# Regrouping the z2 projection of a gMLP layer: nine groups of eight 512-column units across row tiles, and a norm by VectorE alone

## The chip, the cores and the metric

The kernel runs on one core of one Trainium2 chip. A core has TensorE (PE, matrix products into PSUM), VectorE (DVE), ScalarE (ACT), GpSimd (POOL) and SyncE (SP, which issues DMA transfers here). The metric is the device time of one execution in microseconds (us). [...]

## The reference

Four layers run one after the other on a sequence of 2048 rows and 576 columns (D): attention (A), gMLP (B), A, B. Each takes the layer-normed input and adds its result to the stream. A is a dilated sliding-window attention and is not touched. B, with F = 4608 and Fh = 2304, is:

```python
z = gelu(x @ w_in)                      # 2048 x 4608, tanh form
z1 = z[..., :Fh]
z2 = layernorm(z[..., Fh:])             # mean and variance over the 2304 columns of a row
g = w_sp @ z2 + b_sp[:, None]           # w_sp is 2048 x 2048
out = (z1 * g) @ w_out                  # back to 576 columns
```

## The kernel before

A gMLP layer (`layer_B`) has three stages. The first, z2, computes the second half of z, its GELU and its layer norm into `Z`, by row tiles of 128 rows (16 of them). The second, `z1` and `gate`, goes over nine blocks (`jj`) of 256 columns: z1 transposed, and then the product of `Z` with the spatial weights `Wq`. The third projects back (`p3`).

The contraction over D = 576 is four chunks of 128 rows and one of 64. The 64-row chunk of two neighbouring 512-column units is done on the two row halves of the TensorE array at once (`tile_position`, rows 0 and 64; the last rows of the input and of the weights are there twice for it).

In the z2 stage `p1_main(i)` handles one row tile. Its 2304 columns are four units of 512 and one of 256. Two tiles of two PSUM banks (tag `H`, two buffers) take the four units, a one-bank tile (tag `PT`, four buffers) takes the 256 columns. The order on TensorE is: the four full chunks of units 0 and 1, then one block with the 64-row chunk of all five units, then the full chunks of units 2, 3 and 4. ScalarE then does three GELUs from PSUM into the row's buffer `zp` (three buffers), each with a running sum (L831). VectorE squares and sums columns 0 to 1535 (L833), ScalarE the other 768 (L835); the squares themselves go into `spare`, a scratch part of the `Z` tile, which lies where buffers of the layer before lay. Small VectorE operations make mean and variance (L838 to L846), POOL raises to the power -1/2 (L848) and makes -mean * rstd (L850).

`p1_norm(i)` writes the normed row into `Z`: VectorE the first 2048 columns (L858), POOL the last 256 (L860). It is called one row late. The tile framework puts the waits in and orders each engine's queue by readiness, so that a queue need not follow the program text; every engine then runs its queue in order.

Within the loop, transposes of the layer norm that the layer before left over (`run_deferred`) are issued ahead of the row that needs them. After row 2 SP issues four transposing loads of `B_w_sp` into `Wq` (L777) and the first w1 block (L799, L801; into `spare` too); after row 6 POOL issues the load of the bias (L873), into memory that held normed rows of the layer before.

The z1 stage (L887 to L926) has the order that matters for comparison: eight units of 512 columns per block, four in two `H` tiles and four in `PT` tiles, full chunks of the first four, one block with the 64-row chunks of all eight, full chunks of the last four. Its output tiles take over the memory of the z2 stage's pool. A `gate` call (L928) runs 16 matmuls over the row tiles of `Z` in order, into a `PT` bank.

Of the kernel before, what the change touches and what calls it, by code (L numbers as in the profile page):

```python
# [10 lines left out]
ALU = mybir.AluOpType  # L11
# [54 lines left out]
class K:  # L66
# [682 lines left out]
    def layer_B(self, li):  # L749
# [28 lines left out]
        cchunks = []  # L778
        c0 = 0
        while c0 < Fh:  # L780
            cn = min(1024, Fh - c0)
            cchunks.append((c0, cn))
            c0 += cn
        ncch = len(cchunks)
        SQ_D = (Fh * 2 // 3) // 256 * 256
        units = []
        for ci, (c0, cn) in enumerate(cchunks):
            for sub in range((cn + 511) // 512):
                units.append((ci, c0, sub, min(512, cn - sub * 512)))
# [12 lines left out]
        zst = {}  # L802

        def p1_main(i):
            zp = p1.tile([P, Fh], bf16, name="zp", bufs=3)
            sums = p1.tile([P, ncch + 2], f32, name="z_sums", bufs=3)
            pzvs = []
            for ci, (c0, cn) in enumerate(cchunks):
                if cn > 512:
                    pzvs.append(self.H_tile("pz")[:].rearrange("p a b -> p (a b)"))  # L810
                else:
                    pzvs.append(self.PT_tile([P, 512], f32, "pzs")[:, :])

            def z_mm(u, c, start, stop):
                ci, c0, sub, w = units[u]
                r0, r1 = (0, P) if c < 4 else (64 * (u % 2), 64 * (u % 2) + 64)
                nc.tensor.matmul(pzvs[ci][:, sub * 512:sub * 512 + w],  # L817
                                 lhsT=self.xnT[r0:r1, c, PADL + i * P:PADL + (i + 1) * P],
                                 rhs=win2(c)[r0:r1, c0 + sub * 512:c0 + sub * 512 + w],
                                 start=start, stop=stop, tile_position=(r0, 0))  # L820
            nu = len(units)
            for u in range(2):
                for c in range(4):
                    z_mm(u, c, c == 0, False)
            for u in range(nu):
                z_mm(u, 4, u >= 2, u < 2)
            for u in range(2, nu):
                for c in range(4):
                    z_mm(u, c, False, c == 3)
            for ci, (c0, cn) in enumerate(cchunks):  # L830
                nc.scalar.activation(out=zp[:, c0:c0 + cn], in_=pzvs[ci][:, 0:cn],  # L831
                                     func=ACT.Gelu_apprx_tanh, accum_out=sums[:, ci:ci + 1])
            nc.vector.tensor_tensor_reduce(out=spare[:, 0:SQ_D], in0=zp[:, 0:SQ_D], in1=zp[:, 0:SQ_D], scale=1.0,  # L833
                                           scalar=0.0, op0=ALU.mult, op1=ALU.add, accum_out=sums[:, ncch:ncch + 1])
            nc.scalar.activation(out=spare[:, SQ_D:Fh], in_=zp[:, SQ_D:Fh], func=ACT.Square,  # L835
                                 accum_out=sums[:, ncch + 1:ncch + 2])
            mean = p1.tile([P, 1], f32, name="z_mean", bufs=3)
            nc.vector.tensor_reduce(out=mean[:], in_=sums[:, 0:ncch], axis=AX.X, op=ALU.add)  # L838
# [4 lines left out]
            sq = p1.tile([P, 1], f32, name="z_sq", bufs=3)  # L843
            nc.vector.tensor_tensor(out=sq[:], in0=sums[:, ncch:ncch + 1], in1=sums[:, ncch + 1:ncch + 2], op=ALU.add)
# [17 lines left out]

        for i in range(NS):
            self.run_deferred(upto_row=(i + 1) * P)
            p1_main(i)
            if i == 0:
                self.run_deferred()
            if i == min(2, NS - 1):
# [216 lines left out]
```

## Time and profile before

| what | us |
|---|---|
| median of 3 runs | 1184.68 (1182.94 to 1186.77) |
| the profiled execution | 1182.29 |
| its span | 1180.5 |
| TensorE busy | 1169.8 |
| z2 of the first gMLP layer, first matmul to first z1 matmul | 127.93 to 204.56 |
| z2 of the second | 709.94 to 786.12 |
| one z1 block with its gates | 35.6 |

In the timelines the columns are start and duration in us, engine, line, operation, output and inputs, array rows and columns, shape, count; in brackets the idle time of the engine ahead of the instruction and what ended it. Matmuls overlap in the record (each is listed with 379 ns for 512 columns, though one starts every 216 ns), so distances between starts are used, not durations. The profiled execution is one; the median is over others.

### The profile page before, as it was taken

The numbers are of one execution on the slowest core, as the hardware profiler recorded it, in microseconds if no ns is written. First come the engines' busy times: TensorE is split into PE (matmuls) and PEld (weight loads), VectorE is DVE, ScalarE is ACT, GpSimd is POOL, SyncE is SP. The second block draws the span as 40 slices with busy tenths as digits, with TensorE's granted clock in tenths as the row PEclk, the third lists the DMA queues.
The fourth block names the chain that finished last, engine by engine and source line by source line (L and its number), as shares of the span: only waits on it lengthen the run. The fifth ranks groups of instructions, "written<-read, shape, count | busy, mean of one in ns | idle before, by whom it ended". The sixth has DMA issues, their size and how long they took to land.

```text
span 1180.5 us, 20534 instructions
## 1 busy us (share of the span) xinstructions
PE 1169.8 (99%) x8406; PEld 622.2 (53%) x8406; DVE 553.0 (47%) x1232; ACT 377.3 (32%) x621; POOL 285.8 (24%) x383
## 2 busy tenths in 40 slices
PE   9999999999999999999999999999999999999998
PEld 5567544444444444457755774444444444444677
DVE  9778677323333322335556896753322333332321
ACT  5588677111110111102257786770111110111000
POOL 4768784000000000001153787830000000000000
PEclk9999999999999999999999999999999999999999
DMA  8999993000000000049645899900000000001332
GB/s 200 199 136 235 197 206 70 23 12 12 12 1 12 12 12 1 18 145 282 170 99 116 201 245 175 223 23 1 12 12 12 12 3 10 12 1 39 114 106 74
DMA packets 179479, 101.57 MB, mean 86 GB/s; under 512 B 135711, under 2 KB 160735, under 8 KB 179384
## 3 DMA queue, kind: packets, MB, share of 16 engines
q1 hardware_dynamic: 166520, 78.50, 31.2%
q0 software_dynamic: 6512, 16.00, 5.2%
q10 hardware_dynamic: 6352, 5.75, 1.6%
q8 instruction: 66, 1.08, 0.4%
q14 instruction: 29, 0.24, 0.1%
HBM read 42.39 MB, written 16.53 MB: 50 GB/s over the span
## 4 chain that ended last, share of the span: by engine, by line
PE 89%; POOL 4%; DMA 2%; DVE 2%; issue 1%; ACT 1%; SPq 0%; POOLq 0%; ACTq 0%; DVEq 0%
PE pg L931 42%; PE po L973 12%; PE pz L817 9%; PE pz L907 6%; PE pz1s L907 6%; PE pp L409 4%; PE pv L386 2%; PE O_ps L464 2%; PE L_ps L444 2%; POOL ln_xn L245 2%; PE pw L509 2%; PE pzs L817 1%; DMA o_slot<-o_t 1%; DMA QK<-win2a 1%; POOL QK L80 1%
## 5 line engine op out<-in xcount | busy, mean ns | idle before, releaser
L931 PE MATMUL pg<-Wq,Z 128*128 128x512 bf16 x2304 | 500.2, 379 | 0.0
L931 PEld LDWEIGHTS <-Z 128*128 128x128 bf16 x2304 | 225.4, 98 | 271.9
L935 DVE TENSOR_TENSOR g_tmp<-pg,ln_xn 128x512 f32<-128x512 f32 x144 | 99.6, 692 | 422.2 <-PE pg L931 422.2
L926 ACT ACTIVATE z1T<-pz 128x1024 bf16<-128x1024 f32 x36 | 34.9, 1020 | 497.4 <-PE pz L907 493.8
L80 POOL DMA_DIRECT2D wout<-in_B_w_out_dram x4 | 4.2, 1062 | 600.8 <-PE pg L931 600.8
L973 PE MATMUL po<-wout,Z 128*128 128x288 bf16 x1152 | 141.4, 286 | 0.0
L453 ACT ACTIVATE P_sb<-L_ps 128x912 bf16<-128x912 f32 (+1 forms) x144 | 125.7, 929 | 36.2 <-PE L_ps L444 35.3
L973 PEld LDWEIGHTS <-Z 128*128 128x128 bf16 x1152 | 112.7, 98 | 28.8
L817 PEld LDWEIGHTS <-xnT 128*128 128x128 bf16 (+1 forms) x800 | 66.5, 97 | 83.3 <-issue 25.6
L936 DVE TENSOR_TENSOR Z<-g_tmp,z1T 128x512 bf16<-128x512 f32 x144 | 99.7, 692 | 13.0 <-DVE g_tmp L935 0.9
L817 PE MATMUL pz<-win2a,xnT 128*128 128x512 bf16 x384 | 104.1, 380 | 1.5 <-ACT zp L831 1.5
L907 PEld LDWEIGHTS <-w 128*128 128x128 bf16 (+1 forms) x640 | 53.8, 97 | 74.0 <-issue 13.6
L409 PE MATMUL pp<-xnT,wqk_sb 128*128 128x512 bf16 x360 | 82.5, 379 | 0.0
L831 ACT ACTIVATE zp<-pz 128x1024 bf16<-128x1024 f32 x64 | 65.5, 1023 | 36.8 <-PE pz L817 31.1
L983 DVE TENSOR_TENSOR x_new<-po,xo 128x288 f32<-128x288 f32 (+1 forms) x64 | 28.8, 456 | 87.7 <-PE po L973 84.0
L907 PE MATMUL pz<-xnT,w 128*128 128x512 bf16 (+1 forms) x320 | 66.5, 380 | 0.0
L907 PE MATMUL pz1s<-xnT,w 128*128 128x512 bf16 (+1 forms) x320 | 66.5, 379 | 0.0
L817 PE MATMUL pz<-win2b,xnT 128*128 128x512 bf16 (+1 forms) x256 | 65.7, 380 | 0.0
L80 POOL DMA_DIRECT2D QK<-stg x81 | 50.9, 633 | 50.9 <-DVE oT L483 17.9
L833 DVE CUSTOM_DVE_ANT_0 Z<-zp 128x1536 bf16<-128x1536 bf16 x32 | 56.9, 1778 | 11.5 <-ACT zp L831 7.1
L386 PE MATMUL pv<-wv_sb,xnT 128*128 128x288 bf16 (+1 forms) x360 | 52.8, 286 | 1.1 <-DVE o_t L471 1.0
L245 POOL TENSOR_SCALAR ln_xn<-x_new,ln_mv,ln_rstd 128x576 bf16<-128x576 f32 x23 | 53.0, 2303 | 2.0
(118 smaller groups left out, 1002.2 us busy)
## 6 DMA issues: line engine op xcount, KB each, us to landing
xres<-x_new SPq DMA_DIRECT2D x48, 288.0 KB
xo<-xres SPq DMA_DIRECT2D x32, 288.0 KB
wout<-in_B_w_out_dram POOLq DMA_DIRECT2D x4, 1296.0 KB, 8.6
xo<-xres SPq DMA_DIRECT2D x8, 576.0 KB
w<-in_B_w_in_dram SPq DMA_DIRECT2D x16, 256.0 KB
QK<-stg POOLq DMA_DIRECT2D x53, 72.0 KB, 4.3
QK<-stg SPq DMA_DIRECT2D x41, 72.0 KB
xo<-in_A_x_dram SPq DMA_DIRECT2D x8, 288.0 KB
```

The source lines that it names most:

```text
L80: return eng.dma_start(out=out, in_=in_)
L245: e.tensor_scalar(out=xn[:nrows, 0:D], in0=x_t[:nrows, :], scalar1=mv[:nrows, 0:1], scalar2=rstd[:nrows, 0:1], op0=ALU.subtract, op1=ALU.mult)
L386: nc.tensor.matmul(pv[:nk, 0:288], lhsT=self.xnT[:, c, KO + q0_(t):KO + q0_(t) + nk], rhs=wv_sb[:, c, hh * 288:(hh + 1) * 288], start=(c = ...
L409: nc.tensor.matmul(pp[:, :], lhsT=w, rhs=self.xnT[:, c, PADL + cc * 512:PADL + (cc + 1) * 512], start=(c == 0), stop=(c == 4))
L453: nc.scalar.activation(out=P_bufs[(2 * s + jp) % 4][:nk, :, :, 0:nq], in_=Lv[:nk, :, :, 0:nq], func=ACT.Exp, scale=scale)
L817: nc.tensor.matmul(pzvs[ci][:, sub * 512:sub * 512 + w], lhsT=self.xnT[r0:r1, c, PADL + i * P:PADL + (i + 1) * P], rhs=win2(c)[r0:r1, c0 + ...
L831: nc.scalar.activation(out=zp[:, c0:c0 + cn], in_=pzvs[ci][:, 0:cn], func=ACT.Gelu_apprx_tanh, accum_out=sums[:, ci:ci + 1])
L907: nc.tensor.matmul(outs[a_], lhsT=w1[r0:r1, c, sub * P:(sub + 1) * P], rhs=self.xnT[r0:r1, c, PADL + q * 512:PADL + (q + 1) * 512], start= ...
L931: nc.tensor.matmul(pg[:, :], lhsT=Z[:, jj, i, sub * P:(sub + 1) * P], rhs=Wq[q][:, i, :], start=(i == 0), stop=(i == NS - 1))
L935: nc.vector.tensor_tensor(out=tmp[:], in0=pg[:, :], in1=bsp[:, qs], op=ALU.add)
L936: nc.vector.tensor_tensor(out=uT(jj)[:, sub, qs], in0=tmp[:], in1=z1Ts[jj, sub][:, qs], op=ALU.mult)
L973: nc.tensor.matmul(acc[hh], lhsT=uT(j // 2)[:, j % 2, i * P:(i + 1) * P], rhs=wouts[j // NJH][:, j % NJH, hh * 288:(hh + 1) * 288], start= ...
```

## The change

The z2 stage no longer goes row by row. For each pair of row tiles the units are put in a row: four units of 512 columns of the first row, one merged unit ("m") that holds the last 256 columns of both rows side by side in one bank, and four units of the second row. The 72 units are taken eight at a time (`groups`), whatever rows they belong to. A group has two `H` tiles with two neighbouring units each, and four `PT` tiles. `p1_group` does the full chunks of the four `H` units, those of the merged unit's first row, one block with all 64-row chunks (the merged unit's two parts on the same row half, one after the other), and the full chunks of the `PT` units, with the merged unit's second row.

The GELUs follow the units, so a row has up to four or five with a running sum each. ScalarE squares only the 256 columns of the merged unit (`SQ_D` is now 2048), VectorE the other 2048, for the last row in two parts. The factor 1/Fh goes into the squares, and the two sums are added in the last small operation. VectorE norms all 2304 columns in one operation; POOL keeps only the power. Statistics of a row are issued when its last unit is done, the norm one row later. The loads of `Wq` and w1 follow group 1, the bias load follows group 3, and all left-over transposes are issued after group 0.

```diff
--- before.py
+++ after.py
@@ -775,18 +775,7 @@
 
         def load_W(q):
             nc.sync.dma_start_transpose(out=Wq[q][:], in_=self.B_w_sp[q * 512:(q + 1) * 512, :])
-        cchunks = []
-        c0 = 0
-        while c0 < Fh:
-            cn = min(1024, Fh - c0)
-            cchunks.append((c0, cn))
-            c0 += cn
-        ncch = len(cchunks)
-        SQ_D = (Fh * 2 // 3) // 256 * 256
-        units = []
-        for ci, (c0, cn) in enumerate(cchunks):
-            for sub in range((cn + 511) // 512):
-                units.append((ci, c0, sub, min(512, cn - sub * 512)))
+        SQ_D = Fh - 256
         bsp = self.bsp
         w1_0 = spare[:, Fh:Fh + 1280].rearrange("p (c n) -> p c n", n=256)
         p2s = []
@@ -799,81 +788,120 @@
             self.dma(w1[:, 0:4, :], self.B_w_in[0:512, cs].rearrange("(c p) n -> p c n", p=P), eng=nc.sync)
             for r in (0, 64):
                 self.dma(w1[r:r + 64, 4, :], self.B_w_in[512:576, cs], eng=nc.sync)
-        zst = {}
-
-        def p1_main(i):
-            zp = p1.tile([P, Fh], bf16, name="zp", bufs=3)
-            sums = p1.tile([P, ncch + 2], f32, name="z_sums", bufs=3)
-            pzvs = []
-            for ci, (c0, cn) in enumerate(cchunks):
-                if cn > 512:
-                    pzvs.append(self.H_tile("pz")[:].rearrange("p a b -> p (a b)"))
-                else:
-                    pzvs.append(self.PT_tile([P, 512], f32, "pzs")[:, :])
-
-            def z_mm(u, c, start, stop):
-                ci, c0, sub, w = units[u]
-                r0, r1 = (0, P) if c < 4 else (64 * (u % 2), 64 * (u % 2) + 64)
-                nc.tensor.matmul(pzvs[ci][:, sub * 512:sub * 512 + w],
-                                 lhsT=self.xnT[r0:r1, c, PADL + i * P:PADL + (i + 1) * P],
-                                 rhs=win2(c)[r0:r1, c0 + sub * 512:c0 + sub * 512 + w],
-                                 start=start, stop=stop, tile_position=(r0, 0))
-            nu = len(units)
-            for u in range(2):
+        zst, zrow = {}, {}
+        npair, MW = Fh // 1024, Fh % 1024
+        assert MW == 256 and NS % 2 == 0
+        stream = []
+        for r in range(0, NS, 2):
+            stream += [(r, w_) for w_ in range(2 * npair)] + [("m", r)] + [(r + 1, w_) for w_ in range(2 * npair)]
+        groups = [stream[k_:k_ + 8] for k_ in range(0, len(stream), 8)]
+        left = {r: 2 * npair + 1 for r in range(NS)}
+
+        def unit_parts(u):
+            if u[0] == "m":
+                return [(u[1], 2 * npair * 512, 0, MW), (u[1] + 1, 2 * npair * 512, MW, MW)]
+            return [(u[0], u[1] * 512, 0, 512)]
+
+        def z_mm(u, out, c, half, start, stop, part=0):
+            r0, r1 = (0, P) if c < 4 else (64 * half, 64 * half + 64)
+            for r, w0, o0, n in unit_parts(u)[part:part + 1]:
+                nc.tensor.matmul(out[:, o0:o0 + n], lhsT=self.xnT[r0:r1, c, PADL + r * P:PADL + (r + 1) * P],
+                                 rhs=win2(c)[r0:r1, w0:w0 + n], start=start, stop=stop, tile_position=(r0, 0))
+
+        def p1_group(units):
+            pairs = [k_ for k_ in range(len(units) - 1) if units[k_][0] != "m" and units[k_][1] % 2 == 0 and
+                     units[k_ + 1] == (units[k_][0], units[k_][1] + 1)][:2]
+            first = [units[k_ + a_] for k_ in pairs for a_ in range(2)]
+            rest = [u for u in units if u not in first]
+            outs, acts = {}, []
+            for k_ in pairs:
+                ht = self.H_tile("pz")[:].rearrange("p a b -> p (a b)")
+                for a_ in range(2):
+                    outs[units[k_ + a_]] = ht[:, a_ * 512:(a_ + 1) * 512]
+                acts.append((units[k_][0], units[k_][1] * 512, ht, 2))
+            for u in rest:
+                outs[u] = pt = self.PT_tile([P, 512], f32, "pzs")[:, :]
+                for r, w0, o0, n in unit_parts(u):
+                    acts.append((r, w0, pt[:, o0:o0 + n], 1))
+            for u in first:
                 for c in range(4):
-                    z_mm(u, c, c == 0, False)
-            for u in range(nu):
-                z_mm(u, 4, u >= 2, u < 2)
-            for u in range(2, nu):
+                    z_mm(u, outs[u], c, 0, c == 0, False)
+            single = [u for u in first + rest if u[0] != "m"]
+            merged = [u for u in rest if u[0] == "m"]
+            for u in merged:
                 for c in range(4):
-                    z_mm(u, c, False, c == 3)
-            for ci, (c0, cn) in enumerate(cchunks):
-                nc.scalar.activation(out=zp[:, c0:c0 + cn], in_=pzvs[ci][:, 0:cn],
-                                     func=ACT.Gelu_apprx_tanh, accum_out=sums[:, ci:ci + 1])
-            nc.vector.tensor_tensor_reduce(out=spare[:, 0:SQ_D], in0=zp[:, 0:SQ_D], in1=zp[:, 0:SQ_D], scale=1.0,
-                                           scalar=0.0, op0=ALU.mult, op1=ALU.add, accum_out=sums[:, ncch:ncch + 1])
-            nc.scalar.activation(out=spare[:, SQ_D:Fh], in_=zp[:, SQ_D:Fh], func=ACT.Square,
-                                 accum_out=sums[:, ncch + 1:ncch + 2])
+                    z_mm(u, outs[u], c, 0, c == 0, False)
+            for k_, u in enumerate(single):
+                z_mm(u, outs[u], 4, k_ % 2, u in rest, u in first)
+            for u in merged:
+                for k_ in range(2):
+                    z_mm(u, outs[u], 4, 1, k_ == 1, k_ == 0, k_)
+            for u in rest:
+                for c in range(4):
+                    z_mm(u, outs[u], c, 0, False, c == 3, 1 if u[0] == "m" else 0)
+            done = []
+            for r, w0, src, n in acts:
+                if r not in zrow:
+                    zrow[r] = [p1.tile([P, Fh], bf16, name="zp", bufs=3),
+                               p1.tile([P, 2 * npair + 4], f32, name="z_sums", bufs=3), 3]
+                zp, sums, k_ = zrow[r]
+                zrow[r][2] += 1
+                w = src.shape[-1]
+                nc.scalar.activation(out=zp[:, w0:w0 + w], in_=src, func=ACT.Gelu_apprx_tanh,
+                                     accum_out=sums[:, k_:k_ + 1])
+                if w0 == SQ_D:
+                    nc.scalar.activation(out=spare[:, SQ_D:Fh], in_=zp[:, SQ_D:Fh], func=ACT.Square,
+                                         scale=Fh ** -0.5, accum_out=sums[:, 0:1])
+                left[r] -= n
+                if left[r] == 0:
+                    done.append(r)
+            return done
+
+        def p1_stats(i):
+            zp, sums, n = zrow.pop(i)
+            cuts = [0, SQ_D // 2, SQ_D] if i == NS - 1 else [0, SQ_D]
+            for k_, (q0, q1) in enumerate(zip(cuts, cuts[1:])):
+                nc.vector.tensor_tensor_reduce(out=spare[:, q0:q1], in0=zp[:, q0:q1], in1=zp[:, q0:q1], scale=1.0 / Fh,
+                                               scalar=0.0, op0=ALU.mult, op1=ALU.add, accum_out=sums[:, 1 + k_:2 + k_])
+            if len(cuts) > 2:
+                nc.vector.tensor_tensor(out=sums[:, 1:2], in0=sums[:, 1:2], in1=sums[:, 2:3], op=ALU.add)
             mean = p1.tile([P, 1], f32, name="z_mean", bufs=3)
-            nc.vector.tensor_reduce(out=mean[:], in_=sums[:, 0:ncch], axis=AX.X, op=ALU.add)
+            nc.vector.tensor_reduce(out=mean[:], in_=sums[:, 3:n], axis=AX.X, op=ALU.add)
             nc.vector.tensor_scalar_mul(out=mean[:], in0=mean[:], scalar1=1.0 / Fh)
             msq = p1.tile([P, 1], f32, name="z_msq", bufs=3)
             nc.vector.scalar_tensor_tensor(out=msq[:], in0=mean[:], scalar=mean[:, 0:1], in1=self.eps_t[:],
                                            op0=ALU.mult, op1=ALU.subtract)
-            sq = p1.tile([P, 1], f32, name="z_sq", bufs=3)
-            nc.vector.tensor_tensor(out=sq[:], in0=sums[:, ncch:ncch + 1], in1=sums[:, ncch + 1:ncch + 2], op=ALU.add)
             rstd = p1.tile([P, 1], f32, name="z_rstd", bufs=3)
-            nc.vector.scalar_tensor_tensor(out=rstd[:], in0=sq[:], scalar=1.0 / Fh, in1=msq[:],
-                                           op0=ALU.mult, op1=ALU.subtract)
+            nc.vector.scalar_tensor_tensor(out=rstd[:], in0=sums[:, 0:1], scalar=sums[:, 1:2], in1=msq[:],
+                                           op0=ALU.add, op1=ALU.subtract)
             nc.gpsimd.tensor_tensor(out=rstd[:], in0=rstd[:], in1=self.neg_half[:], op=ALU.pow)
-            nmr = p1.tile([P, 1], f32, name="z_nmr", bufs=3)
-            nc.gpsimd.tensor_scalar(out=nmr[:], in0=mean[:], scalar1=rstd[:, 0:1], scalar2=-1.0,
-                                    op0=ALU.mult, op1=ALU.mult)
-            zst[i] = (zp, mean, rstd, nmr)
+            zst[i] = (zp, mean, rstd)
 
         def p1_norm(i):
-            zp, mean, rstd, nmr = zst.pop(i)
-            nb = NB - 1
+            zp, mean, rstd = zst.pop(i)
             zv = zp[:].rearrange("p (b c) -> p b c", c=256)
-            nc.vector.tensor_scalar(out=Z[:, 0:nb, i, :], in0=zv[:, 0:nb, :], scalar1=mean[:, 0:1],
+            nc.vector.tensor_scalar(out=Z[:, 0:NB, i, :], in0=zv, scalar1=mean[:, 0:1],
                                     scalar2=rstd[:, 0:1], op0=ALU.subtract, op1=ALU.mult)
-            nc.gpsimd.tensor_scalar(out=Z[:, nb, i, :], in0=zv[:, nb, :], scalar1=rstd[:, 0:1],
-                                    scalar2=nmr[:, 0:1], op0=ALU.mult, op1=ALU.add)
-
-        for i in range(NS):
-            self.run_deferred(upto_row=(i + 1) * P)
-            p1_main(i)
-            if i == 0:
+
+        waiting = []
+        for k_, units in enumerate(groups):
+            self.run_deferred(upto_row=(max(r for u in units for r, _, _, _ in unit_parts(u)) + 1) * P)
+            done = p1_group(units)
+            if k_ == 0:
                 self.run_deferred()
-            if i == min(2, NS - 1):
+            if k_ == 1:
                 for q in range(NQ):
                     load_W(q)
                 load_w1(0)
-            if i == min(6, NS - 1):
+            if k_ == 3:
                 self.dma(bsp, self.B_b_sp.partition_broadcast(P), eng=nc.gpsimd)
-            if i >= 1:
-                p1_norm(i - 1)
-        p1_norm(NS - 1)
+            for r in done:
+                p1_stats(r)
+                waiting.append(r)
+                if len(waiting) > 1:
+                    p1_norm(waiting.pop(0))
+        while waiting:
+            p1_norm(waiting.pop(0))
         p1_cm.__exit__(None, None, None)
         self.right["pf_cm"].__exit__(None, None, None)
         self.right = None
```

## The prediction

> **What bounds the kernel now.** I read the page first: busy shares, then the chain of waits, then the windows and timelines of the two z2 stages.
>
> ```profile
> PE 1169.8 (99%) x8406; PEld 622.2 (53%) x8406; DVE 553.0 (47%) x1232; ACT 377.3 (32%) x621; POOL 285.8 (24%) x383
> PE 89%; POOL 4%; DMA 2%; DVE 2%; issue 1%; ACT 1%; SPq 0%; POOLq 0%; ACTq 0%; DVEq 0%
> ```
>
> TensorE is the path (89% of the chain). "99% busy" hides what matters, since matmuls overlap in this record; the distance from one start to the next is what counts. So I read z2 as steps of the chain, beside z1 (the next stage), which already works in the pattern that the change brings to z2. Columns: start, us, what.
>
> ```profile
> 153.68 2.27 PE pz L817 x12
> 156.05 1.83 PE pz L817 x8
> 158.32 2.27 PE pz L817 x12
> ...
> 204.72 3.99 PE pz L907 x20
> 208.71 3.99 PE pz1s L907 x20
> ```
>
> A row of z2 takes 158.32 - 153.68 = 4.64 us and holds one block of 64-row matmuls. A z1 step has eight 512-column units and also one such block, and takes 3.99 + 3.99 = 7.98 us. Inside a row (TensorE's timeline):
>
> ```profile
> 164.31 0.38 PE L817 MATMUL pz<-win2b,xnT 128*128 128x512 bf16 x1
> 164.62 0.61 PE L817 MATMUL pz<-win2b,xnT 64*128 64x512 bf16 x4
> 165.06 0.27 PE L817 MATMUL pzs<-win2b,xnT 64*128 64x256 bf16 x1
> 165.27 0.82 PE L817 MATMUL pz<-win2a,xnT 128*128 128x512 bf16 x3
> 166.14 0.81 PE L817 MATMUL pz<-win2a,xnT 128*128 128x512 bf16 x3
> ```
>
> Four full matmuls take 166.14 - 165.27 = 0.865, so a slot of 512 columns is 0.216 us. From the last full start (164.31) to the first 64-row start (164.62) is 0.31: entering the block costs 0.095 beyond the slot. From 165.06 to 165.27 is 0.21 for a matmul of 256 columns (0.108): leaving costs another 0.10. Between, two pairs side by side take 0.44. Each block thus costs about 0.20 us of switching.
>
> Two waits also lie on the path, one per layer:
>
> ```profile
> 139.60 0.81 PE L817 MATMUL pz<-win2a,xnT 128*128 128x512 bf16 x3 [0.98 <-ACT zp L831]
> 137.61 0.84 ACT L835 ACTIVATE Z<-zp 128x768 bf16<-128x768 bf16 x1 [2.55 <-DMA xnT<-stg]
> 730.45 0.81 PE L817 MATMUL pz<-win2a,xnT 128*128 128x512 bf16 x3 [0.53 <-ACT zp L831]
> 729.28 1.02 ACT L831 ACTIVATE zp<-pz 128x1024 bf16<-128x1024 f32 x1 [1.96 <-DVE z_sq L844]
> 727.29 1.95 POOL L860 TENSOR_SCALAR Z<-zp,z_rstd,z_nmr 128x256 bf16<-128x256 bf16 x1
> ```
>
> In the first layer ScalarE's Square waits for a transpose out of memory that `spare` takes over; the GELU behind it frees the next PSUM tile late. In the second, GELU of row 3 waits for the `zp` buffer of row 0, which VectorE and then POOL's norm (727.29 + 1.95 = 729.24) still hold. By start times TensorE loses 1.1 and 0.7 us there.
>
> **The change part by part.** The sum is against the profiled execution, 1182.29 us (span 1180.5 and 1.8 around it). The median shown is 1184.68, or 2.39 more, which I add at the end.
>
> *TensorE, steady.* Before, a row is 20 slots of 512, a lone 64-row matmul of half a slot, and a block: 20.5 x 0.216 + 0.20 = 4.63 (4.64 seen); 16 rows are 74.24 us. After, a group has 32 full slots (the merged unit's are eight of 256 columns) and four pairs: the seventh 512 unit lies beside the two halves of the merged one. 36 x 0.216 + 0.20 = 7.98, which is z1's own time. Nine groups: 71.8. Saved 2.4 us a layer: four slots (0.87) and seven blocks (1.4). Matmuls stay 400 a layer, weight loads too (98 ns under slots of 108 or 216). Bounds on the merged unit: 0, as it fits z1's pattern, to one more slot in eight groups (1.7 a layer) if its halves do not run beside the 512. I take 0: the lone 64-row matmul of 256 columns before starts 0.21 after the pair ahead and costs no extra slot.
>
> [...]
>
> *The first wait.* Group 0 ends at 127.93 + 1.23 (output matmuls of the layer before, in between) + 7.98 = 137.1. ScalarE reaches the first Square near 136.4 and stays blocked to 137.6. Behind it are Square 0.47, the second half's GELU 0.5, Square 0.47, and three GELUs of 512 (0.60 apart in z1, which reads no accumulator; 0.66 with one, an estimate from 0.97 and 1.00 for 1024): the one-bank tiles come free at 138.7, 139.8, 140.5, 141.2. Group 1 first needs such a bank 16 slots in, at 140.6 (that of 139.8), the last at 141.8. TensorE waits 0; bounds 0 and today's 1.1. I take 0.3, as the margins are under a microsecond.
>
> *The second wait.* POOL's norm of 256 columns goes (32 x 0.56 to 1.95 us, POOL only), with L850's 0.79. Row 3 now waits for row 0's VectorE norm alone. POOL's power came at 725.71, behind the bias DMA of L873, which waits for the last transpose; the norm then ends near 727.3, and ScalarE would want the buffer about 727.2. What is late next is VectorE's backlog of three rows, which reaches the one-bank GELUs of group 2. Bounds 0 and 1.2; I take 0.5.
>
> *VectorE.* Sum of squares: 1.68 start to start for 1536, so 2.24 in proportion for 2048, a little less if part is fixed; I take 2.2. Small operations 1.0, less the `z_sq` add: 0.78. Norm 0.73 for 2048, between 0.73 and 0.82 for 2304; 0.80. Together 3.8 a row, or 4.45 if it waits each time for POOL's power (0.67 from the last small operation to the norm, in all 32 rows). A row's share of a group is 71.8 / 16 = 4.49. So it is hidden, thinly.
>
> *ScalarE.* A group: two GELUs of 1024 (1.0 each), three of 512 (0.66), two of 256 (0.5), two Squares (0.47, between 0.38 and 0.84): 5.9 us of 7.98. It ends some 2.7 after TensorE's group, and the next group needs the last bank after 3.46: margin 0.75.
>
> *End of a stage.* Row 15 is complete 2.5 us after TensorE leaves z2. Two sums of 1.15, small operations, power and two norms put its Z at about +7 us (+5 today). The first gate reads row 15 at 7.98 + 15 x 0.216 = +11.2. Row 14's norm ends at about +6.3, which may hold the third z1 GELU 0.4 us if its output takes over that row's buffer; the gate's bank has 1.5 us. Cost 0, bounds 0 and 1.5.
>
> *DMA issues.* SP's four transposes of `B_w_sp` and three loads of w1 move from after row 2 (13.9 us in) to after group 1 (16.0); they filled SP from 141.7 to 183.9, and the gate starts near 209. The last row's transpose moves past group 0, but POOL finishes its input at 139.6, later than that. POOL's bias load moves from after row 6 (32.5 us) to after group 3 (31.9). All cost nothing.
>
> Sum: layer 1, -2.4 - 1.1 + 0.3 = -3.2; layer 2, -2.4 - 0.7 + 0.5 = -2.6. Total -5.8, of which I keep -5.7, leaving 0.1 to the stage ends: 1176.6 profiled, 1179.0 median.
>
> **The rivals.**
> (1) VectorE's in-order queue eats part of the gain: two rows now complete together, and a norm waits behind the next row's 2.2 us sum while a GELU needs that `zp` buffer (three exist). For: the margins of 0.75 and of 4.49 against 4.45. Against: 3.8 if the power is covered. A norm behind a whole sum and its small operations is 3.0 late, 2.2 beyond the margin; once a layer that is 4.4, less the 0.8 of waits counted already: 1182.6.
> (2) Slower, by one mechanism: POOL's power is held while VectorE works. POOL's 256-column norm took 0.56 alone and 1.95 beside the sum of squares. If the norm of a row always waits for such a power, a row costs 4.45 plus the hold. Up to 4.49 it is free; at 4.7 z2 takes 75.3, as today with its waits (74.24 + 1.1 and + 0.7), and beyond that it is slower. With half a microsecond of hold it is 4.95, or 79.2 a layer, 3.9 and 4.3 over today: 1192.9. Against: no power waited so far, and the next row's small operations can cover it. [...]
> (3) The merged unit's halves do not pair: +1.7 a layer, 1182.4.
>
> **How the numbers follow.** Forecast 0.66, rival 1 0.14, rival 2 0.10, rival 3 0.10. A measurement can tell about 0.3% (3.6 us) from no change. The forecast with waits at their lower bounds gives -6.6 (1178.1); two microseconds for the spread of the runs give 1176. Above, it runs with the upper bounds of the waits (+1.5), the stage end (+1) and that spread to 1184, where rivals 1 and 3 lie; 1185 leaves rival 2. Faster takes most of the forecast and little of rivals 1 and 3 (0.70), same the rest of these (0.18), slower rival 2 and a little of rival 1 (0.12).
>
> **What would show it.** Groups of z2 7.98 apart; z1 starting 3.2 and then 5.8 us earlier; 18 blocks of 64-row matmuls in both z2 stages together, not 32; no POOL norm; no wait of TensorE over 0.6 in z2. It is wrong if z2's groups are over 8.2 apart, if TensorE waits for GELUs, or if the first gate halts at row 14 or 15.

## The result

The changed kernel takes 1202.0 us (median of five runs, 1200.9 to 1205.2), the kernel before 1184.77 (five runs beside it, 1182.9 to 1186.8). The ratio is 1.0147, with a 95% interval of 1.0127 to 1.0167: slower by 17 us, where the prediction said 1179.0, between 1176 and 1185. The profiled execution took 1200.93 us, with a span of 1199.1.

The page of the changed kernel, its busy line and its chain of waits by engine:

```profile
PE 1172.0 (98%) x8406; PEld 624.0 (52%) x8406; DVE 583.0 (49%) x1206; ACT 359.8 (30%) x677; POOL 215.9 (18%) x319
...
PE 77%; DVE 11%; POOL 5%; DMA 2%; ACT 2%; issue 2%; POOLq 0%; DVEq 0%; ACTq 0%
```

TensorE's work is what it was (1172.0 us busy against 1169.8, as many matmuls), but its share of the chain fell from 89% to 77%, and VectorE's rose from 2% to 11%. POOL is relieved as announced (215.9 us, before 285.8). Where VectorE came into the chain is seen in the groups by line and in the chain of the end of the first z2 stage (columns: start, us, what):

```profile
L883 DVE TENSOR_SCALAR Z<-zp,z_mean,z_rstd 128x2304 bf16<-128x2304 bf16 x32 | 46.4, 1470 | 24.1 <-POOL z_rstd L877 24.1
```

```profile
199.10 2.20 DVE Z L864
...
202.29 0.56 POOL z_rstd L877
...
202.87 1.47 DVE Z L883
204.35 2.20 DVE Z L864
...
207.46 0.56 POOL z_rstd L877
...
208.05 1.47 DVE Z L883
209.52 2.20 DVE Z L864
...
215.33 1.48 DVE Z L883
...
216.89 2.44 ACT z1T L954 x3
219.33 0.04 issue
219.37 2.72 PE pg L959 x6
```

The norm of 2304 columns takes 1.470 us a time. The norm of 2048 took 0.813 in the kernel before:

```profile
L858 DVE TENSOR_SCALAR Z<-zp,z_mean,z_rstd 128x2048 bf16<-128x2048 bf16 x32 | 26.0, 813 | 31.0 <-POOL z_rstd L848 31.0
```

A row on VectorE is now a serial loop: sum 2.20, small operations, POOL's power (0.73 with the way there and back), norm 1.47, and then the next sum; from 199.10 to 204.35 is 5.25, from 204.35 to 209.52 is 5.17. TensorE, where nothing holds it, delivers a row every 4.5 us (a group starts at 138.82 and the next at 146.82 in the run with the even cut below, 8.00 us for 16/9 of a row). So VectorE falls behind through the stage, its norm of row 14 ends at 216.8, ScalarE's first z1 GELU starts right behind it, and the first gate starts when the third of these GELUs (2.44 us for the three) has freed its PSUM bank.

TensorE's timeline at the end of the first stage in the kernel before, and at both ends in the changed kernel (in brackets the idle time ahead, and what ended it):

```profile
212.54 27.79 PE L931 MATMUL pg<-Wq,Z 128*128 128x512 bf16 x128
240.17 4.16 PE L907 MATMUL pz<-xnT,w 128*128 128x512 bf16 x20
```

```profile
205.60 4.16 PE L935 MATMUL pz<-xnT,Z 128*128 128x512 bf16 x20
209.59 4.15 PE L935 MATMUL pz1s<-xnT,Z 64*128 64x512 bf16 x20
219.37 29.73 PE L959 MATMUL pg<-Wq,Z 128*128 128x512 bf16 x128 [5.63 <-ACT z1T L954]
248.94 4.16 PE L935 MATMUL pz<-xnT,w 128*128 128x512 bf16 x20
...
810.63 29.36 PE L959 MATMUL pg<-Wq,Z 128*128 128x512 bf16 x128 [5.63 <-ACT z1T L954]
839.83 4.16 PE L935 MATMUL pz<-xnT,w 128*128 128x512 bf16 x20
```

By distances between starts, in us (first z2 matmul, first z1 matmul, first gate, next z1):

| | z2 | z1 to first gate | its gates | sum |
|---|---|---|---|---|
| before, first layer | 76.63 | 7.98 | 27.63 | 112.24 |
| after, first layer | 76.48 | 13.77 | 29.57 | 119.82 |
| before, second layer | 76.18 | 7.99 | 27.62 | 111.79 |
| after, second layer | 77.78 | 13.78 | 29.20 | 120.76 |

The stages lose 7.6 and 9.0 us. That is 16.6 of the 18.6 between the two profiled executions; the first z2 starts 1.2 later, behind code that was not changed, and 0.9 is spread over the rest. Two things are to be seen. The gain of z2 is gone inside z2, by waits of TensorE for GELUs whose `zp` buffer VectorE still held. From the list of waits (who waited for whom, us in total, times, the longest):

```profile
ACT zp L850 <- DVE Z L883: 47.0, 16, 5.5
PE pz L808 <- ACT zp L850: 5.1, 7, 1.4
```

And the gates, in which nothing was changed, take 1.6 to 1.9 us longer. Windows of the changed kernel around the first gate show why; PEclk, the granted TensorE clock, is the third number from the right:

```profile
214.00:217.00 3.00, 0.00 (x0) 0.00 (x0) 2.50 (x10) 0.11 (x1) 0.55 (x1) 0.92 0.00 0
217.00:219.00 2.00, 0.00 (x0) 0.00 (x0) 1.34 (x1) 2.00 (x3) 0.55 (x1) 0.50 0.00 0
219.00:223.00 4.00, 3.63 (x9) 1.28 (x9) 0.13 (x1) 1.79 (x4) 0.00 (x0) 0.50 0.45 131
223.00:224.00 1.00, 1.00 (x5) 0.43 (x4) 0.00 (x0) 0.00 (x0) 0.00 (x0) 0.83 0.46 131
224.00:228.00 4.00, 4.00 (x20) 1.77 (x19) 1.39 (x2) 0.00 (x0) 0.00 (x0) 1.00 0.00 0
```

Here the clock falls to 0.50 while TensorE stands, and it is back at 1.00 only some 4 us after the gate has begun.

### The profile page after: what moved, and what is told of

Same layout as the page of the kernel before. It is cut to its first block, busy times and chain, and to the rows that moved or that the text cites. A ratio compares the mean times of both kernels' runs of the same rounds, so it can differ in the third digit from the quotient of the medians.

```text
span 1199.1 us, 20476 instructions
## 1 busy us (share of the span) xinstructions
PE 1172.0 (98%) x8406; PEld 624.0 (52%) x8406; DVE 583.0 (49%) x1206; ACT 359.8 (30%) x677; POOL 215.9 (18%) x319
## 4 chain that ended last, share of the span: by engine, by line
PE 77%; DVE 11%; POOL 5%; DMA 2%; ACT 2%; issue 2%; POOLq 0%; DVEq 0%; ACTq 0%
PE pg L959 42%; PE po L1001 12%; PE pp L409 5%; PE pz L935 5%; PE pz1s L935 5%; DVE Z L864 5%; DVE Z L883 3%; PE pv L386 2%; POOL ln_xn L245 2%; PE O_ps L464 2%; PE L_ps L444 2%; PE pw L509 2%; POOL z_rstd L877 1%; DMA QK<-win2a 1%; DMA o_slot<-o_t 1%
## 5 line engine op out<-in xcount | busy, mean ns | idle before, releaser
L864 DVE CUSTOM_DVE_ANT_0 Z<-zp 128x2048 bf16<-128x2048 bf16 (+1 forms) x34 | 73.4, 2159 | 10.3 <-ACT zp L850 5.5
L808 PE MATMUL pz<-win2a,xnT 128*128 128x512 bf16 x216 | 58.4, 379 | 5.1 <-ACT zp L850 5.1
L808 PE MATMUL pzs<-win2a,xnT 128*128 128x512 bf16 (+1 forms) x264 | 60.5, 341 | 0.0
L883 DVE TENSOR_SCALAR Z<-zp,z_mean,z_rstd 128x2304 bf16<-128x2304 bf16 x32 | 46.4, 1470 | 24.1 <-POOL z_rstd L877 24.1
```

The costliest lines, as they stand in the source:

```text
L808: nc.tensor.matmul(out[:, o0:o0 + n], lhsT=self.xnT[r0:r1, c, PADL + r * P:PADL + (r + 1) * P], rhs=win2(c)[r0:r1, w0:w0 + n], start=start ...
L864: nc.vector.tensor_tensor_reduce(out=spare[:, q0:q1], in0=zp[:, q0:q1], in1=zp[:, q0:q1], scale=1.0 / Fh, scalar=0.0, op0=ALU.mult, op1=AL ...
L883: nc.vector.tensor_scalar(out=Z[:, 0:NB, i, :], in0=zv, scalar1=mean[:, 0:1], scalar2=rstd[:, 0:1], op0=ALU.subtract, op1=ALU.mult)
```

## The experiments

The first theory: the norm's 1.47 us comes from how it is addressed, because its destination has nine blocks, an odd number; with a faster norm the rest of the prediction holds. Rivals: it is the length, or the regrouping is what costs, or POOL's part was no burden and taking it away gained nothing.

**The norm with an even cut.** Same data, written as 2 x 9 blocks of 128 columns:

```diff
-            zv = zp[:].rearrange("p (b c) -> p b c", c=256)
-            nc.vector.tensor_scalar(out=Z[:, 0:NB, i, :], in0=zv, scalar1=mean[:, 0:1],
-                                    scalar2=rstd[:, 0:1], op0=ALU.subtract, op1=ALU.mult)
+            zv = zp[:].rearrange("p (b h c) -> p h b c", h=2, c=128)
+            nc.vector.tensor_scalar(out=Z[:, 0:NB, i, :].rearrange("p b (h c) -> p h b c", h=2), in0=zv,
+                                    scalar1=mean[:, 0:1], scalar2=rstd[:, 0:1], op0=ALU.subtract, op1=ALU.mult)
```

> The changed kernel; the one norm of 2304 columns is only addressed differently, as 2 x 9 x 128 in place of 9 x 256. Theory A (the norm's price: 1.47 us in the changed kernel where 0.80 was assumed, because nine blocks are an odd outermost count): the norm takes 0.85 to 0.95, VectorE's row falls from 5.18 to about 4.6, the stop of the first gate (5.6 us in each layer) goes, time 1178 to 1185. Theory B (the grouping: rows that end in pairs, three zp buffers and VectorE's queue order, whatever the norm costs): the stops stay, 1195 or more. If the odd count is not the cause, the norm stays at 1.47 and the time at 1202.

Measured: 1184.6 us, ratio 1.000 (0.9986 to 1.0013). The norm's group in this run:

```profile
L883 DVE TENSOR_SCALAR Z<-zp,z_mean,z_rstd 128x2304 bf16<-128x2304 bf16 x32 | 28.1, 879 | 27.0 <-POOL z_rstd L877 26.4
```

0.879 us in place of 1.470, and 17.4 us of the total: all that the change had lost. z2 takes 73.2 us in both layers, 3.4 and 3.0 less than before the change. But that gain does not reach the total. It is given back behind z2, by the timeline of TensorE:

```profile
213.06 27.79 PE L959 MATMUL pg<-Wq,Z 128*128 128x512 bf16 x128 [2.14 <-ACT z1T L954]
...
795.36 29.47 PE L959 MATMUL pg<-Wq,Z 128*128 128x512 bf16 x128 [2.42 <-ACT z1T L954]
```

The first gate waits 2.14 and 2.42 us, and behind the second wait the clock is halved again (0.50 from 796 to 799; 29.3 us of gates from start to start). Together 6.3 us, nearly the whole gain of 6.4. So the way the norm is cut is the cause of the loss, and a second cause keeps the gain from showing.

**The nine groups with the old norm** (VectorE 2048 columns, POOL 256, and POOL's `z_nmr` for it):

```diff
-            nc.vector.tensor_scalar(out=Z[:, 0:NB, i, :], in0=zv, scalar1=mean[:, 0:1],
+            nb = NB - 1
+            nc.vector.tensor_scalar(out=Z[:, 0:nb, i, :], in0=zv[:, 0:nb, :], scalar1=mean[:, 0:1],
                                     scalar2=rstd[:, 0:1], op0=ALU.subtract, op1=ALU.mult)
+            nc.gpsimd.tensor_scalar(out=Z[:, nb, i, :], in0=zv[:, nb, :], scalar1=rstd[:, 0:1],
+                                    scalar2=nmr[:, 0:1], op0=ALU.mult, op1=ALU.add)
```

> The changed kernel with the norm of before: VectorE 2048 columns in one operation, POOL the last 256 with its scale and bias step. Groups and sums stay. Theory A: VectorE's norm is 0.81 again, z2 is 72 to 73 us a layer, time 1179 to 1187 (POOL's 0.6 to 2.0 us hold zp longer). Theory B: 1195 or more.

Measured: 1194.75 us, ratio 1.008 (1.006 to 1.0101). Regrouping with the old norm is slower than before by 10 us. The total lies where the second theory began (1195), but what TensorE comes to wait for is POOL's norm, whose hold the first theory had put at 0.6 to 2.0 us. POOL's and VectorE's timelines in this run:

```profile
202.87 2.48 POOL L889 TENSOR_SCALAR Z<-zp,z_rstd,z_nmr 128x256 bf16<-128x256 bf16 x1
...
207.33 2.50 POOL L889 TENSOR_SCALAR Z<-zp,z_rstd,z_nmr 128x256 bf16<-128x256 bf16 x1
...
214.15 0.56 POOL L889 TENSOR_SCALAR Z<-zp,z_rstd,z_nmr 128x256 bf16<-128x256 bf16 x1
```

```profile
202.63 2.29 DVE L864 CUSTOM_DVE_ANT_0 Z<-zp 128x2048 bf16<-128x2048 bf16 x1
...
207.11 2.29 DVE L864 CUSTOM_DVE_ANT_0 Z<-zp 128x2048 bf16<-128x2048 bf16 x1
```

POOL's norm of 256 columns takes 0.56 us in most rows, and 2.5 when it starts beside a sum of squares of VectorE: it ends 0.43 us after that sum. GELUs wait 47.8 us in all for a `zp` that POOL still holds (20 times; 1.4 us, 3 times, in the kernel before). So in the new order taking POOL's part away was worth it. That part is not dearer than before on average: the norm takes 1.04 us (1.39 before) and `z_nmr` 1.17 (0.79 before), though the longest norm is 2.5 in place of 2.0. What the regrouping changes is how long a GELU has to wait for it.

**The old order with the new norm.** The kernel before, row by row, with the nine blocks normed by VectorE alone (POOL's `z_nmr` goes too):

```diff
-            nb = NB - 1
-            nc.vector.tensor_scalar(out=Z[:, 0:nb, i, :], in0=zv[:, 0:nb, :], scalar1=mean[:, 0:1],
+            nc.vector.tensor_scalar(out=Z[:, 0:NB, i, :], in0=zv, scalar1=mean[:, 0:1],
                                     scalar2=rstd[:, 0:1], op0=ALU.subtract, op1=ALU.mult)
-            nc.gpsimd.tensor_scalar(out=Z[:, nb, i, :], in0=zv[:, nb, :], scalar1=rstd[:, 0:1],
-                                    scalar2=nmr[:, 0:1], op0=ALU.mult, op1=ALU.add)
```

> The kernel before with nothing changed but the norm: VectorE alone, 9 x 256 in one operation, row by row as before. Theory A: the norm takes 1.47; VectorE's row is 1.68 + 1.02 + 0.67 + 1.39 = 4.76 over TensorE's 4.64, so it falls behind by 0.1 a row and about 2 at the end of z2; slower than before by 2 to 8 us, 1187 to 1193. Theory B: the norm alone costs nothing, 1183 to 1187.

Measured: 1188.17 us, ratio 1.0028 (1.0016 to 1.0039). The slow norm in place of the shared one costs some 3.5 us here (1.8 of it in the two stages, by their starts), and in place of the fast one about 17 there. VectorE's timeline in this run:

```profile
202.17 1.47 DVE L854 TENSOR_SCALAR Z<-zp,z_mean,z_rstd 128x2304 bf16<-128x2304 bf16 x1 [0.73 <-POOL z_rstd L848]
...
206.82 1.47 DVE L854 TENSOR_SCALAR Z<-zp,z_mean,z_rstd 128x2304 bf16<-128x2304 bf16 x1 [0.73 <-POOL z_rstd L848]
```

A row is 206.82 - 202.17 = 4.65 us, since its sum covers 1536 columns only; TensorE delivers a row every 4.64. VectorE just keeps up. With the regrouping the square sum gets longer as well, and TensorE's share for a row falls to 4.5; together they take VectorE well past it.

**Seven blocks and two.** The norm as two operations, to tell the odd count from the length:

```diff
-            nc.vector.tensor_scalar(out=Z[:, 0:NB, i, :], in0=zv, scalar1=mean[:, 0:1],
-                                    scalar2=rstd[:, 0:1], op0=ALU.subtract, op1=ALU.mult)
+            for b0, b1 in ((0, 7), (7, NB)):
+                nc.vector.tensor_scalar(out=Z[:, b0:b1, i, :], in0=zv[:, b0:b1, :], scalar1=mean[:, 0:1],
+                                        scalar2=rstd[:, 0:1], op0=ALU.subtract, op1=ALU.mult)
```

> The changed kernel with the norm in two VectorE operations, of seven and of two blocks. It tells what makes the nine blocks dear. [...] If a length over 2048 does: seven blocks take 0.75, two 0.4, together 1.0 to 1.1 start to start, and the time is 1180 to 1190.

Measured: 1203.62 us, ratio 1.0165 (1.0144 to 1.0185). The two groups:

```profile
L884 DVE TENSOR_SCALAR Z<-zp,z_mean,z_rstd 128x1792 bf16<-128x1792 bf16 x32 | 38.5, 1204 | 23.6 <-POOL z_rstd L877 23.6
...
L884 DVE TENSOR_SCALAR Z<-zp,z_mean,z_rstd 128x512 bf16<-128x512 bf16 x32 | 12.9, 404 | 0.0
```

Seven blocks, 1792 columns, take 1.204 us, longer than the 0.813 of eight blocks. It isn't the length. Between the odd counts (1792 and 2304) a column costs (1470 - 1204) / 512 = 0.52 ns; between the even ones (512 and 2048) (813 - 404) / 1536 = 0.27 ns. What is left of each is 0.27 us. In these shapes a column takes about twice as long with an odd count of blocks (0.52 against 0.27 ns).

The second theory, for the gain that was given back: `z1T` takes over the `zp` buffer of row 14, so that the first z1 GELU waits for that row's norm; put elsewhere, it does not wait. Rival: VectorE's backlog is met anyway, by the weight load that reads row 15, or the place of the buffers is a gain by itself.

**The even cut, with z1's pool elsewhere.** The pool of `z1T`, `w1` and `g_tmp` is opened on the right-hand side, over the `win2a` and `win2b` that TensorE has finished with:

```diff
-        p2_cm = pool("p2", 2)
+        p2_cm = tc.tile_pool(name=f"B{li}_p2", bufs=2, side="right", reuse_waits="tile")
```

> The changed kernel with two edits: the norm addressed as 2 x 9 x 128 columns (as in the run that took 1184.6), and the pool that holds z1T, w1 and g_tmp opened on the right-hand side of SBUF, over the freed win2a and win2b, so that z1's GELUs take over no zp buffer. Theory (the 1184.6 of that run still carries z1T's wait for row 14's norm): TensorE no longer stands before the first gate (2.14 us in the first layer, 2.42 in the second), and the gates of the second layer run at a granted clock of 1.00 from the start (27.6 instead of 29.3, so 1.7 to 1.85 more). 1184.6 - 2.14 - 2.42 - 1.8 = 1178.2, between 1177 and 1180. Row 15's norm ends at 212.2, the first gate would need it at 210.9 + 3.2 = 214.1. Rival (the wait was for VectorE's backlog itself, and moves to the weight load that reads row 15): 1182 to 1185, with a halt of 2 us inside the first gate.

Measured: 1178.58 us, ratio 0.9962 (0.9949 to 0.9974), against 1178.2 expected. It is faster than both kernels, by 0.4% against the kernel before. TensorE's timeline:

```profile
210.17 27.79 PE L959 MATMUL pg<-Wq,Z 128*128 128x512 bf16 x125 [0.26 <-ACT z1T L954]
...
790.37 27.79 PE L959 MATMUL pg<-Wq,Z 128*128 128x512 bf16 x125
```

But for 0.26 us in the first layer the waits are gone, and so are the slow gates. Row 15's norm ends at 209.54 + 0.88 = 210.4, ahead of the gate that reads it from 213.4 on.

**The changed kernel, with only that pool elsewhere** (the same line, norm left at nine blocks).

> The changed kernel with its norm of 9 blocks of 256 as it is (1.47 us), and only z1's pool moved to the right-hand side. Theory: of the 13.8 us from z1's start to the first gate, the wait of 5.63 goes; the first gate starts at once and halts at row 15, whose norm ends at 219.1, where the gate would need it at 213.6 + 3.2 = 216.8: 2.3 us. Saved 3.3 us a layer: 1202.0 - 6.6 = 1195.4; if a halt of 2.3 leaves the granted clock at 1.00 (2.14 did, 2.42 did not) another 1.8 a layer, 1191.8. Rival A (all of the loss is VectorE's row being longer than its share, wherever the buffers lie): 1200 to 1203. Rival B (the buffers alone are the loss): 1180 to 1185.

Measured: 1194.79 us, ratio 1.0108 (1.0089 to 1.0126). Neither rival: some 6 to 7 us of the loss go with the buffers (7.2 by the two medians, 5.7 with each against the kernel before beside it), and 10 to 11.5 stay. The total is the 1195.4 of the theory, but by luck: one layer saves more than the 3.3 us expected and the other less. In the second layer it went as expected, with the halt inside the gate:

```profile
802.75 2.97 PE L959 MATMUL pg<-Wq,Z 128*128 128x512 bf16 x13
806.02 0.39 PE L959 MATMUL pg<-Wq,Z 128*128 128x512 bf16 x1 [0.30 <-DVE Z L883]
808.35 24.56 PE L959 MATMUL pg<-Wq,Z 128*128 128x512 bf16 x111 [1.94 <-DVE Z L883]
```

From z1's start to the next z1 it is 37.98 us, 5.0 less than in the changed kernel. In the first layer only 0.8 is saved, because something else took the wait's place; VectorE's norm of row 14 and ScalarE's timeline there:

```profile
213.25 1.47 DVE L883 TENSOR_SCALAR Z<-zp,z_mean,z_rstd 128x2304 bf16<-128x2304 bf16 x1 [0.39 <-POOL z_rstd L877]
214.76 0.53 ACTq L80 DMA_DIRECT2D wqk_sb<-in_A_wqkv_dram  x1
215.57 0.60 ACT L954 ACTIVATE z1T<-pz1s 128x512 bf16<-128x512 f32 x1 [6.11 <-DVE z_rstd L875]
```

With z1's pool moved, the loads of the next attention layer's weights, which ScalarE issues, are scheduled between the second and the third z1 GELU, and the first of them is issued 0.04 us after VectorE's norm of row 14 has ended (213.25 + 1.47 = 214.72). The profile puts the GELU's wait down to the last `z_rstd`, but two other runs agree with the norm: in the run with both edits row 14's norm ends at 207.81 + 0.88 = 208.69 and the load is issued at 208.72; in the run with the old norm and this pool (below) POOL's part of it ends at 213.66 + 0.56 = 214.22 and the load is issued at 214.25, while the last power runs on to 214.73. So it looks as if the load's tile has taken over the very `zp` buffer that `z1T` left; no run moved that tile, so this is not shown. In the run with both edits the norm is 6 us earlier, and the gate loses only the 0.26 us above.

**The control: the kernel before, with only that pool elsewhere** (the same line).

> The kernel before with only z1's pool moved to the right-hand side. It is the control of the run with both edits. Theory: in the kernel before TensorE does not stand between z2 and the first gate (7.98 us from z1's start to the gate in both layers), so there is nothing to remove: 1184.7, within 0.2%. Rival (the place of z1's buffers gains by itself, for instance by w1's loads): it gains the same 6 us, 1178.

Measured: 1184.55 us, beside 1183.26 for the kernel before in these runs: ratio 1.0015 (1.0004 to 1.0025). The place of the buffers gains nothing by itself.

**The nine groups with the old norm, and that pool elsewhere** (the edits of the second and the fifth run together).

> The nine groups with the norm of the kernel before (VectorE 2048 columns, POOL 256), 1194.75 us by itself, and z1's pool on the right-hand side. Theory: the wait of 3.48 before the first gate goes in both layers, and with it the halved clock after it (gates 29.3 and 28.9 against 27.6, so 1.7 and 1.3); row 15's norm on POOL ends at 216.8, the first gate would need it at 213.7 + 3.2 = 217.0. 1194.75 - 2 x 3.48 - 3.0 = 1184.8, as the kernel before: regrouping then gains nothing without a VectorE-only norm, since z2 itself takes as long (76.2 us) by POOL's late norms. Rival (the wait moves inside the gate): 1188 to 1194.

Measured: 1189.09 us, ratio 1.0051 (1.0037 to 1.0065), 4 us more than expected. The second layer behaves (7.98 us from z1 to a first gate that doesn't wait). In the first, the moved load again holds the GELUs, now behind POOL's part of row 14's norm: the gate waits 2.45 us, and its gates take 29.3. That is the missing 4 us. The number lies in the rival's range, but the wait stands before the gate and not inside it, as the rival had it. Without these 4 us the run would be level with the kernel before; that a norm shared with POOL makes regrouping worthless fits this, but is an inference.

**An odd count on both sides.** The even cut had changed source and destination at once. Here `zp` has its nine rows of 256 at a pitch of 264, so that the source, too, can only be read as 9 x 256 (the GELUs and the squares use the padded rows as well, by lines not shown):

```diff
-                    zrow[r] = [p1.tile([P, Fh], bf16, name="zp", bufs=3),
+                    zrow[r] = [p1.tile([P, NB, 264], bf16, name="zp", bufs=3),
...
-            zv = zp[:].rearrange("p (b c) -> p b c", c=256)
+            zv = zp[:, :, 0:256]
```

> The changed kernel with zp kept as nine rows of 256 columns at a pitch of 264, so that the norm's source can't be merged into one run of 2304 columns: source and destination are then both 9 x 256 in one operation, an odd count that is equal on both sides. Theory A (what slows the norm is that source and destination are cut differently, 1 x 2304 against 9 x 256): the norm takes 0.88 us as with 2 x 9 x 128, VectorE's row 4.6, and the kernel 1184.6 within 2 us, like the run with the even cut. Theory B (any odd count of blocks on the destination is slow): the norm stays at 1.47 and the kernel at 1200 to 1204. The sum of squares reads the padded rows too; if that makes it longer than 2.2 us, the row and the time rise by sixteen times that in each layer under either theory.

Measured: 1185.52 us, ratio 1.0009 (0.9995 to 1.0024). The norm and the sum in this run:

```profile
L866 DVE CUSTOM_DVE_ANT_1 Z<-zp 128x2048 bf16<-128x2048 bf16 x30 | 68.4, 2281 | 10.4 <-ACT zp L850 10.1
L885 DVE TENSOR_SCALAR Z<-zp,z_mean,z_rstd 128x2304 bf16<-128x2304 bf16 x32 | 29.7, 944 | 26.3 <-POOL z_rstd L879 26.3
```

0.944 us with nine blocks on both sides. So the odd count alone is not slow here; it is slow (1.470 us) where the source is cut otherwise. In the changed kernel `zp` is one run of 2304 columns without gaps, which can be written as 1 x 2304 (that it is so written I infer from this run), against a destination of nine blocks. The 0.065 more than with the even cut is about what a tenth block would cost at the even rate (an estimate: 256 x 0.27 ns = 0.07 us); where it comes from no run shows.

The total agrees with the first theory too, within its 2 us. The sum of squares did not get longer on padded rows: 2.281 us, 2.284 in the changed kernel.

Side by side, the same 2304 columns took 0.879 us with 2 x 9 x 128 on both sides, 0.944 with 9 x 256 on both, and 1.470 with 9 x 256 against an unbroken source; against such a source the odd and the even counts of blocks differ by 0.52 / 0.27 = 1.9 in what a column costs. Why the cut sets the rate no run shows.

## Why the prediction was wrong

*"VectorE", the norm: the step that failed.* It took the norm of 2304 columns as 0.80 us, "between 0.73 and 0.82", by scaling the row of the same operation on 2048 columns (0.73 from its start to the next, 0.813 long). That row has eight blocks. One block more changed the rate, not only the length: 1.39 us measured from start to start (202.87 to 204.26), 1.470 long. With the even cut it is 0.80 from start to start (198.33 to 199.13), the very figure taken. The other terms of the step nearly hold: the sum 2.2 (2.2 taken), and small operations and power together 1.58 (1.45 taken), and VectorE does wait for the power in most rows (24 of 32). So a row is 5.2 us instead of 3.8 or 4.45, against the 4.49 that the step itself gives as the share. Sixteen rows at 0.7 too much are 11 us of backlog a layer. TensorE pays for it partly in z2 (some 3.4 us in the first layer: 76.48, less 1.24 of output matmuls that lie between and 71.8; 4.7 in the second) and partly before the first gate (5.63). That term, mis-sized by 0.59 us, accounts for the sign: with the even cut the loss is gone. The small operations, mis-sized by 0.13, leave that run's row at 4.58 (198.33 to 202.91), still 0.1 over the share, so that "hidden, thinly" was not quite true for a fast norm either.

*"End of a stage": wrong in two points.* It put row 14's norm at +6.3 and had it hold, at most, the third z1 GELU. By the record it holds the first. The first three GELUs take 2.44 us and the gate is due 7.98 us after z1's start, so the first has to start about 5.5 us after it for the gate not to wait, and the wait is the norm's end less that: 11.2 - 5.5 in the changed kernel (5.63 seen), and 7.7 - 5.5 with the even cut (2.14 seen). Even at the predicted +6.3 it would have cost 0.8 a layer. The price of 0 was too low by 2.1 and 2.4 even with the even cut, plus the clock; its bound of 1.5 a layer did not reach that, and the stated range took in only 1 of it for both layers.

*The clock behind a wait was not counted at all.* A wait of TensorE was priced at its length. Behind the 5.63 us the gates take 1.9 and 1.6 us longer, and so a third more is to be added.

*"TensorE, steady": right.* In the run with the even cut z2 goes from 129.57 to 202.77, 73.20 us, and in the second layer from 711.59 to 784.79, 73.20 too. Less 1.24 for the output matmuls that lie between it is 72.0, where nine groups were put at 71.8. The merged unit's halves pair with the seventh unit; rival 3 falls.

*"The first wait" and "the second wait": both go*, and with the norm repaired nothing takes their place: TensorE has no listed wait for a GELU in either z2 stage of the run with the even cut. The 0.3 and 0.5 that I kept were not needed, and the zeros of "ScalarE" and "DMA issues" hold in that run by the same sign.

*Rival 2 had the threshold and the wrong cause.* It said that a row over 4.7 us makes the kernel slower, and gave 1192.9 for 4.95. By its working 5.2 gives 1184.68 + 2 x (16 x 5.2 - 75.1) = 1200.9, close to the 1202.0 measured. But it had POOL's power held by VectorE, and in the changed kernel it was not: 0.54 to 0.59 us in all 32 rows. (In the three runs with a fast norm of 2304 columns it takes 0.64 to 0.66 on average against 0.55; see the last section.) The sum comes out nearly right although most of the loss lies behind z2, because a backlog of VectorE is paid there as well as in z2; the clock is not in it.

*Rival 1* (a `zp` buffer still held) is how the backlog reached TensorE within z2: GELUs waited 47.0 us in all, 16 times, for VectorE's norm. At 1182.6 it was priced for a fast norm.

With both failing steps undone, the sum of the prediction nearly stands. It forecast 5.7 us less for the change. The change with the norm cut evenly and z1's buffers elsewhere takes 4.7 less than the kernel before beside it (1178.58 against 1183.26). That 1178.6 is so near the forecast 1179.0 is in part luck, as the kernel before ran 1.4 faster there.

## What to carry to other kernels

Before a VectorE operation is lengthened, look at the number of blocks on both sides, not only at the columns (here the same 2304 bf16 columns took 0.879, 0.944 or 1.470 us by their cut): scale a duration only between shapes that are cut alike, and try an odd destination with a cut that is even or the same on both sides. Before a stage is shortened, find which buffer the next stage's first outputs take over and who lets go of it last; here another engine was behind at the end of the stage, and 6.3 us of a gain of 6.4 were handed back there. And a wait of TensorE may cost more than its length: here the shortest that did was 2.42 us, with gates of 29.31 us behind it in place of 27.62.

## What the runs showed of the hardware

The halved clock was not expected. Each row here is one stage end, with TensorE's wait ahead of the first gate and the distance from that gate to the next z1:

| TensorE's wait, us | gates, us | which run |
|---|---|---|
| 0 to 0.32 | 27.6 | before, both layers; old order with new norm, first; both edits, both; old norm and pool elsewhere, second; the control, both |
| 1.79 | 27.62 | old order with new norm, second layer |
| 2.14 | 27.62 | even cut, first |
| 2.42 | 29.31 | even cut, second |
| 2.45 | 29.31 | old norm and pool elsewhere, first |
| 2.86 | 29.31 | odd on both sides, second |
| 2.89 | 27.62 | odd on both sides, first |
| 3.48 | 29.31, 28.94 | nine groups with the old norm, both |
| 4.42 | 29.31, 30.51 | seven and two, both |
| 4.53 | 29.84 | nine blocks and pool elsewhere, first |
| 5.63 | 29.57, 29.20 | the changed kernel, both |

Up to 2.14 us no wait costs more than itself, from 3.48 on each one does, by 1.3 to 2.9 us, and between them it goes either way: 2.86 does and 2.89 does not, in one execution. (A halt of 1.94 us inside a gate, nine blocks and pool elsewhere, second layer, left the clock at 1.00 too.) Windows of the run with the odd count on both sides, in its first and its second layer:

```profile
216.00:219.00 3.00, 3.00 (x16) 1.34 (x15) 0.05 (x1) 0.72 (x2) 0.00 (x0) 1.00 0.68 196
```

```profile
797.00:798.00 1.00, 0.47 (x3) 0.23 (x3) 0.00 (x0) 1.00 (x3) 0.00 (x0) 0.98 0.01 2
798.00:801.00 3.00, 3.00 (x9) 1.07 (x8) 0.00 (x0) 0.95 (x2) 0.00 (x0) 0.50 0.70 204
```

The granted clock is 1.00 in the one and 0.50 in the other, with 16 against 9 matmuls started in 3 us. In the second layer the gate begins at 797.53, and the clock stands at 0.98 in that microsecond: it falls only when TensorE is already at work again. What decides between the two after waits of 2.42 to 2.89 us no run shows.

The other is that the time of POOL's work differed with what VectorE did beside it. With the old norm in nine groups, 256 columns took 0.56 us or, beside the sum of squares, 2.48 to 2.50, and `z_nmr`, one column, 1.17 on average (0.79 in the kernel before). POOL's power of one column took 0.55 also where VectorE's slow norm of 1.47 us ran beside it (the changed kernel, the norm from 153.06 on), but 1.00 us beside the fast one (even cut, from 170.30, two norms from 170.37 to 172.20). On average the power took 0.662 us with the even cut, 0.659 with both edits and 0.643 with the odd count on both sides, the three runs with a fast norm of 2304 columns, against 0.551 in the changed kernel. Why no run shows.
